# Cross-covariance attention and maxout FFN: k loaded ahead of q, norms taken during the gram, weights in halves, first v transposed on TensorE, split tail

## The chip, the cores and the metric

One core of one Trainium2 chip. The metric is the device time of one execution in microseconds (us). Each kernel ran several times on the same chip as the kernel before. The experiments were run in three calls on three chips, each beside the kernel before, which took 614.36 us beside the first four experiments, 614.28 beside the next four and 615.03 beside the last version and its base. A run's time is about 1.7 to 2.2 us longer than the span in its trace (614.43 against 612.3 us for the profiled run of the kernel before). Inside the traces I therefore compare spans and moments, and between kernels medians of the times.

The engines are PE (TensorE; PEld is its weight load), DVE (VectorE), ACT (ScalarE), POOL (GpSimd, which issues the loads here) and SP (which issues the stores and the DMA transposes). SPq is SP's queue.

## The reference, cut to what matters

```
# q, k, v: (4, 6144, 256) f32
qn = q / norm(q, axis=1);  kn = k / norm(k, axis=1)
s  = kn^T @ qn / tau                    # (4, 256, 256)
a  = softmax(s, axis=-1)
x  = v @ a                              # (4*6144, 256)
h  = max(x @ w1, x @ w2, x @ w3)        # d_ff = 768
out = h @ w_out
```

The kernel never forms x. Per batch it computes `aw_m = a @ w_m` once and then `h = max(v @ aw_m)`. So a batch needs all of q and k (the "gram") and a short chain of small operations (the softmax) before its first useful matmul on v.

## The kernel before

The parts that matter, with cuts marked (...):

```python
    make_identity(nc, ident)
    for w in [2, 2] + [4] * 10 + [2, 2]:   # q and k pieces in turn
        load_qk(0, g0, w); g0 += w
    # whole w1, w2, w3, then v0, v1, wo, v2: all on POOL's queue
    ...
def gram(b):                               # per pair of groups tp, per half j:
    # q_j x k (256 columns), q_j x q_j (128), k_j x k_j (128), all into one PSUM bank
def softmax_t(ps):
    # DVE dkm = diag(k x k) -> PE kb = ones x dkm -> ACT Ln, Exp -> rkb (1/norm of k)
    # DVE n2q = diag(q x q) -> ACT Ln, Exp -> rq
    # DVE e_in = gram * rkb -> ACT et = Exp(e_in * rq)
    ...
def v_transpose(gi):
    SP.dma_start_transpose(out=vt, in_=v_sb)

for ch in range(NCH):                      # NCH = 12 chunks of 512 tokens per batch
    load_v(gi + 3)                         # POOL; 4 v buffers
    v_transpose(gi + 2)                    # SP
    if more and 1 <= ch < 9:
        load_qk(b + 1, (ch - 1) * 6, 6)    # POOL, next batch
    for fc in range(FC):                   # 6 blocks of 128 columns of d_ff
        h_block(gi, aw, fc)                # 6 matmuls, ACT copy, two DVE max
        if ch == NCH - 1 and more and fc == 0:
            et = softmax_t(ps)
        # output matmuls of the chunk before, between the blocks
    # gram(b + 1) after chunk 10; aw of b + 1 after chunk 11
```

A block's six matmuls fill three of six PSUM banks. ACT copies the first bank to SBUF, DVE takes the maximum with the second and then with the third.

## Time and profile before

| | before |
|---|---|
| time, median of 3 | 614.6 us (614.44 to 615.2) |
| span of the trace | 612.3 us |
| PE busy | 580.5 us (95%) |
| end of the first gram (its last matmul starts at 37.12) | 37.4 us |
| first matmul on v (h_ps) | 50.13 us |
| PE idle at each of three batch boundaries | 2.1 us |

PE is busy 95% of the span. As long as its own work stays the same, time can come only from where it is idle or slow: the head, the boundaries and the tail. The first view is PE's own list of waits over the whole run: who was waited for, us in total, times, longest.

```profile
PE gram L148 <- DMA k_sb<-in_k_dram: 14.3, 12, 5.2
PE kb_ps L163 <- DVE dkm L160: 5.9, 4, 1.8
PE h_ps L237 <- DMA vt_sb<-v_sb: 3.6, 1, 3.6
PE rs_ps L193 <- ACT et L181: 2.2, 2, 2.0
PE o_ps L256 <- DVE ht_sb L242: 0.9, 1, 0.9
PE h_ps L237 <- ACT s_mx L240: 0.8, 3, 0.3
```

The first gram waits for k. The norm chain (dkm, kb) is waited for four times, once in each batch. The first transposed v costs one wait of 3.6 us, and the tail 0.9. The last line is a wait of 0.3 us at each boundary for the ACT copy (s_mx); with the 1.8 for dkm it makes up the 2.1 us of the table.

The timeline of the head shows the order (start, duration, engine, line, operation, count; in brackets the idle time before and what ended it):

```profile
37.79 0.70 PE L163 MATMUL kb_ps<-dkm,ones_f 128*128 128x256 f32 x2 [0.38 <-DVE dkm L160]
...
40.98 5.57 PE L205 MATMUL ew_ps<-w_sb,et 128*128 128x384 bf16 x24
...
43.20 8.52 SPq L225 DMA_TRANSPOSE vt_sb<-v_sb  x4
...
50.13 12.22 PE L237 MATMUL h_ps<-vt_sb,aw_sb 128*128 128x512 bf16 x48 [3.58 <-DMA vt_sb<-v_sb]
...
50.65 0.53 POOL L108 DMA_DIRECT2D v_sb<-in_v_dram  x1 [13.49 <-DMA vt_sb<-v_sb]
```

POOL stood still for 13.5 us, because the load of the fifth v tile (v4) needs the buffer of v0, which is free only when the DMA transpose of v0 has read it. The next batch's q and k loads stand behind v4 in POOL's order.

The view by stretches at the second boundary (stretch, its length, then busy us and instructions of PE, PEld, DVE, ACT and POOL, granted clock, DMA share, GB/s):

```profile
320.00:330.00 10.00, 7.90 (x45) 4.30 (x44) 7.15 (x17) 4.42 (x11) 0.00 (x0) 1.00 0.01 2
```

PE is idle for 2.1 of these 10 us. The timeline of the tail:

```profile
605.11 0.69 DVE L242 TENSOR_TENSOR ht_sb<-h_ps,s_mx 128x512 bf16<-128x512 f32 x1
...
605.86 2.25 PE L256 MATMUL o_ps<-wo_sb,ht_sb 128*128 128x256 bf16 x19 [0.86 <-DVE ht_sb L242]
...
608.14 0.60 ACT L259 ACTIVATE o_sb<-o_ps 128x512 f32<-128x512 f32 x1 [0.66 <-PE o_ps L256]
```

19 of the last 24 output matmuls run after the last ht, because the first output tile needs it and PE works in order.

### The profile page before, as it was taken

The numbers are of one execution on the slowest core, as the hardware profiler recorded it, in microseconds if no ns is written. First come the engines' busy times: TensorE is split into PE (matmuls) and PEld (weight loads), VectorE is DVE, ScalarE is ACT, GpSimd is POOL, SyncE is SP. The second block draws the span as 40 slices with busy tenths as digits, with TensorE's granted clock in tenths as the row PEclk, the third lists the DMA queues.
The fourth block names the chain that finished last, engine by engine and source line by source line (L and its number), as shares of the span: only waits on it lengthen the run. The fifth ranks groups of instructions, "written<-read, shape, count | busy, mean of one in ns | idle before, by whom it ended". The sixth has DMA issues, their size and how long they took to land. (4 is left out here: it accounts for less than half of the span.)

```text
span 612.3 us, 9533 instructions
## 1 busy us (share of the span) xinstructions
PE 580.5 (95%) x3576; PEld 351.5 (57%) x3576; DVE 409.8 (67%) x638; ACT 241.4 (39%) x433; POOL 69.6 (11%) x134
## 2 busy tenths in 40 slices
PE   3777999999989999999999999999998999999996
PEld 3753555555766555555585555555585555555554
DVE  0025778787627887877716878777735787777774
ACT  0033444444225444444405444444423544444442
POOL 6433012100100211100110211110000000000000
PEclk9988999999999999999999999999999999999999
DMA  8999999944732978854570787895440434433111
GB/s 71 105 176 147 153 96 168 155 117 87 147 43 78 127 133 127 130 114 121 101 107 35 118 127 102 146 148 102 121 87 1 109 81 87 121 69 104 53 69 70
DMA packets 77102, 65.11 MB, mean 106 GB/s; under 512 B 53504, under 2 KB 64768, under 8 KB 77056
## 3 DMA queue, kind: packets, MB, share of 16 engines
q0 software_dynamic: 19456, 26.75, 38.4%
q1 hardware_dynamic: 57600, 37.76, 24.6%
q8 instruction: 28, 0.46, 0.3%
q14 instruction: 18, 0.15, 0.1%
HBM read 78.64 MB, written 25.17 MB: 170 GB/s over the span
## 5 line engine op out<-in xcount | busy, mean ns | idle before, releaser
L237 PE MATMUL h_ps<-vt_sb,aw_sb 128*128 128x512 bf16 x1728 | 404.7, 380 | 4.4 <-DMA vt_sb<-v_sb 3.6
L241 DVE TENSOR_TENSOR s_mx<-h_ps,s_mx 128x512 bf16<-128x512 f32 x288 | 198.0, 687 | 116.3 <-ACT s_mx L240 115.2
L237 PEld LDWEIGHTS <-aw_sb 128*128 128x128 bf16 x1728 | 169.1, 98 | 172.5 <-issue 4.5
L240 ACT ACTIVATE s_mx<-h_ps 128x512 bf16<-128x512 f32 x288 | 171.1, 595 | 225.0 <-PE h_ps L237 222.9
L242 DVE TENSOR_TENSOR ht_sb<-h_ps,s_mx 128x512 bf16<-128x512 f32 x288 | 199.2, 692 | 30.0
L256 PE MATMUL o_ps<-wo_sb,ht_sb 128*128 128x256 bf16 x1152 | 155.4, 273 | 0.9 <-DVE ht_sb L242 0.9
L256 PEld LDWEIGHTS <-ht_sb 128*128 128x128 bf16 x1152 | 112.6, 98 | 51.9 <-DVE ht_sb L242 1.1
L259 ACT ACTIVATE o_sb<-o_ps 128x512 f32<-128x512 f32 x96 | 57.3, 597 | 92.1 <-PE o_ps L256 89.5
L108 POOL DMA_DIRECT2D v_sb<-in_v_dram x48 | 25.7, 536 | 443.5 <-DMA vt_sb<-v_sb 441.3
L148 PE MATMUL gram<-k_sb,q_sb 128*128 128x512 fp8e4 x192 | 56.4, 330 | 14.3 <-DMA k_sb<-in_k_dram 14.3
L152 PE MATMUL gram<-k_sb 128*128 128x256 fp8e4 x192 | 47.0, 245 | 0.0
L150 PE MATMUL gram<-q_sb 128*128 128x256 fp8e4 x192 | 46.6, 243 | 0.0
L150 PEld LDWEIGHTS <-q_sb 128*128 128x256 fp8e4 x192 | 28.0, 146 | 8.1 <-issue 7.9
L148 PEld LDWEIGHTS <-q_sb 128*128 128x256 fp8e4 x192 | 27.9, 145 | 7.2 <-DMA q_sb<-in_q_dram 6.9
L152 PEld LDWEIGHTS <-k_sb 128*128 128x256 fp8e4 x192 | 30.6, 159 | 0.0
L160 DVE TENSOR_TENSOR dkm<-gram,ident 128x128 f32<-128x128 f32 x8 | 2.0, 283 | 36.1 <-PE gram L152 36.1
L100 POOL DMA_DIRECT2D k_sb<-in_k_dram x38 | 20.9, 551 | 12.3 <-DMA k_sb<-in_k_dram 6.1
L99 POOL DMA_DIRECT2D q_sb<-in_q_dram x38 | 20.9, 551 | 8.5 <-DMA q_sb<-in_q_dram 7.1
L211 DVE TENSOR_SCALAR aw_sb<-ew_ps,rinv 128x384 bf16<-128x384 f32 x24 | 14.6, 617 | 7.0 <-PE ew_ps L205 6.4
L171 ACT ACTIVATE lnk<-kb_ps 128x256 f32<-128x256 f32 x4 | 1.5, 384 | 44.8 <-PE kb_ps L163 44.8
L205 PE MATMUL ew_ps<-w_sb,et 128*128 128x384 bf16 x96 | 18.2, 346 | 0.0
L208 ACT ACTIVATE aw_sb<-ew_ps,rinv 128x384 bf16<-128x384 f32 x24 | 13.0, 580 | 3.5 <-PE ew_ps L205 3.1
(24 smaller groups left out, 34.4 us busy)
## 6 DMA issues: line engine op xcount, KB each, us to landing
out_dram<-o_sb SPq DMA_DIRECT2D x48, 512.0 KB, 2.9
v_sb<-in_v_dram POOLq DMA_DIRECT2D x48, 256.0 KB, 3.9
q_sb<-in_q_dram POOLq DMA_DIRECT2D x24, 192.0 KB, 5.9
k_sb<-in_k_dram POOLq DMA_DIRECT2D x24, 192.0 KB, 7.6
q_sb<-in_q_dram POOLq DMA_DIRECT2D x10, 128.0 KB, 9.7
k_sb<-in_k_dram POOLq DMA_DIRECT2D x10, 128.0 KB, 9.7
w_sb<-in_moe_w_dram POOLq DMA_DIRECT2D x3, 384.0 KB, 8.6
vt_sb<-v_sb SPq DMA_TRANSPOSE x48, 3.9
```

The lines of the kernel that those rows point to most:

```text
L99: POOL.dma_start(out=qt[:, g0:g0 + w, :], in_=q_r[b][:, g0:g0 + w, :])
L100: POOL.dma_start(out=kt[:, g0:g0 + w, :], in_=k_r[b][:, g0:g0 + w, :])
L108: POOL.dma_start(out=t, in_=v_r[gi // NCH, gi % NCH])
L148: PE.matmul(ps[j][:, 0:C], lhsT=qt[:, tsl, jsl], rhs=kt[:, tsl, :], start=(tp == 0), stop=last, perf_mode=DR, skip_group_check=True)
L150: PE.matmul(ps[j][:, C:C + P], lhsT=qt[:, tsl, jsl], rhs=qt[:, tsl, jsl], start=False, stop=last, perf_mode=DR, skip_group_check=True)
L152: PE.matmul(ps[j][:, C + P:C + 2 * P], lhsT=kt[:, tsl, jsl], rhs=kt[:, tsl, jsl], start=False, stop=last, perf_mode=DR, skip_group_check=True)
L237: PE.matmul(t.rearrange("p (t n) -> p t n", t=TPC), lhsT=aw[m][:, ic, fsl], rhs=vt[:, :, ic, :], start=(ic == 0), stop=(ic == CC - 1))
L240: ACT.activation(out=s_mx, in_=hp[0], func=AF.Copy)
L241: DVE.tensor_tensor(out=s_mx, in0=hp[1], in1=s_mx, op=ALU.max)
L242: DVE.tensor_tensor(out=ht[:, fc, :], in0=hp[2], in1=s_mx, op=ALU.max)
L256: PE.matmul(st["ps"][:, half], lhsT=ht[:, fc, t * P:(t + 1) * P], rhs=wo_sb[:, fc, :], start=(fc == 0), stop=(fc == FC - 1))
L259: ACT.activation(out=st["o"][:, t - 1:t + 1, :].rearrange("p t d -> p (t d)"), in_=st["ps"], func=AF.Copy)
```

## The change

Its intent: shorten the head (k first, its norms taken while q arrives; half of the weights and the first v ahead of the rest; the first v transposed on PE; PE kept busy with matmuls on zeros during the first softmax), take the norm chain off the path at the boundaries, and shorten the tail. The diff, cut to its core:

```diff
-    for w in [2, 2] + [4] * 10 + [2, 2]:
-        load_qk(0, g0, w)
+    for load, widths in ((load_k, [4, 4] + [8] * 5), (load_q, [8] * 5 + [4, 2, 2])):
+        ... # identity made after the first two k loads
+    load_w(0)          # left halves of w1, w2, w3
     load_v(0)
+    load_w(1)          # right halves
     load_v(1)
@@ gram
+        kk = htile("kk")
+        for tp in range(NG // 2):      # all k x k first
+            ...
+        # DVE: dkm = diag(kk)
         ps = [xtile(f"gram{j}") for j in range(CC)]
         for tp in range(NG // 2):      # q x k and q x q only
+            if tp == 11:
+                # PE kb = ones x dkm; ACT Ln, Exp -> rkb
+        return ps, rkb
@@ softmax_t: n2q, rq, e_in, et only
+    def v_transpose_pe(gi):
+        vt_ps = xtile("vt_ps", cols=TPC * C, dtype=BF16)
+        for i in range(TPC * CC):
+            PE.matmul(vt_ps[...], lhsT=v_sb[...], rhs=ident, is_transpose=True, ...)
+        ACT.activation(...)            # copy the first half to vt
+        DVE.tensor_copy(...)           # and the second
@@ head
-    v_transpose(0)
-    v_transpose(1)
     ps = gram(0)
-    et = softmax_t(ps)
+    for i in range(8):
+        PE.matmul(warm_ps, lhsT=ident, rhs=warm, ...)      # zeros
+    et = softmax_t(*ps)
     rinv = rowsums(et)
-    aw_half(et, rinv, aw, 0)
-    aw_half(et, rinv, aw, 1)
+    aw_half(et, rinv, aw, 0, [2], lambda: v_transpose_pe(0))
+    v_transpose(1)
@@ chunk 0
+    gaps[0].insert(0, lambda: aw_half(et, rinv, aw, 1))    # after block 0
@@ tail
-    for f in pending:
-        f()
+    o_last(B * NCH - 1)   # 20 matmuls on blocks 0..4 first, then 4 on block 5;
+                          # ACT and DVE copy, stores from ACT and SP
```

More of the change, by code (lines that the diff above doesn't have):

```diff
@@ L95, in alloc_qk, with load_k, load_q @@
                  qk_pool.tile([P, NG, C], FP8, name="k_sb", tag="k"))
-    def load_qk(b, g0, w):
-        qt, kt = qk[b]
-        POOL.dma_start(out=qt[:, g0:g0 + w, :], in_=q_r[b][:, g0:g0 + w, :])
-        POOL.dma_start(out=kt[:, g0:g0 + w, :], in_=k_r[b][:, g0:g0 + w, :])
+    def load_k(b, g0, w):
+        POOL.dma_start(out=qk[b][1][:, g0:g0 + w, :], in_=k_r[b][:, g0:g0 + w, :])
+    def load_q(b, g0, w):
+        POOL.dma_start(out=qk[b][0][:, g0:g0 + w, :], in_=q_r[b][:, g0:g0 + w, :])
     v_tiles = {}
@@ L109, in load_v, with load_w @@
         v_tiles[gi] = t
-    ident = consts.tile([P, P], BF16, name="ident")
-    make_identity(nc, ident)
     alloc_qk(0)
-    g0 = 0
-    for w in [2, 2] + [4] * 10 + [2, 2]:
-        load_qk(0, g0, w)
-        g0 += w
-    w_sb = []
-    for i, w in enumerate(w_list):
-        wt = consts.tile([P, CC, d_ff], BF16, name=f"w{i}_sb")
-        POOL.dma_start(out=wt, in_=w.rearrange("(cc p) f -> p cc f", p=P))
-        w_sb.append(wt)
+    for load, widths in ((load_k, [4, 4] + [8] * 5), (load_q, [8] * 5 + [4, 2, 2])):
+        g0 = 0
+        for w in widths:
+            load(0, g0, w)
+            g0 += w
+            if load is load_k and g0 == 8:
+                ident = consts.tile([P, P], BF16, name="ident")
+                make_identity(nc, ident)
+    w_sb = [consts.tile([P, CC, d_ff], BF16, name=f"w{i}_sb") for i in range(3)]
+    def load_w(fh):
+        fsl = slice(fh * FH, (fh + 1) * FH)
+        for wt, w in zip(w_sb, w_list):
+            POOL.dma_start(out=wt[:, :, fsl], in_=w.rearrange("(cc p) f -> p cc f", p=P)[:, :, fsl])
+    load_w(0)
     load_v(0)
+    load_w(1)
     load_v(1)
@@ L134 @@
     DVE.memset(ones_c, 1.0)
+    warm = consts.tile([P, CHUNK], BF16, name="warm")
+    DVE.memset(warm, 0.0)
     neg_ln_tau = -math.log(float(tau)) if float(tau) != 1.0 else 0.0
@@ L141, in gram @@
         qt, kt = qk[b]
+        kk = htile("kk")
+        for tp in range(NG // 2):
+            tsl = slice(2 * tp, 2 * tp + 2)
+            for j in range(CC):
+                jsl = slice(j * P, (j + 1) * P)
+                PE.matmul(kk[:, jsl], lhsT=kt[:, tsl, jsl], rhs=kt[:, tsl, jsl], start=(tp == 0 and j == 0),
+                          stop=(tp == NG // 2 - 1), perf_mode=DR, skip_group_check=True)
+        dkm = sm.tile([P, C], FP32, name="dkm")
+        for j in range(CC):
+            jsl = slice(j * P, (j + 1) * P)
+            DVE.tensor_tensor(out=dkm[:, jsl], in0=kk[:, jsl], in1=ident, op=ALU.mult)
         ps = [xtile(f"gram{j}") for j in range(CC)]
@@ L151, in gram, with softmax_t @@
                           start=False, stop=last, perf_mode=DR, skip_group_check=True)
-                PE.matmul(ps[j][:, C + P:C + 2 * P], lhsT=kt[:, tsl, jsl], rhs=kt[:, tsl, jsl],
-                          start=False, stop=last, perf_mode=DR, skip_group_check=True)
-        return ps
-    def softmax_t(ps):
-        dkm = sm.tile([P, C], FP32, name="dkm")
-        for j in range(CC):
-            DVE.tensor_tensor(out=dkm[:, j * P:(j + 1) * P], in0=ps[j][:, C + P:C + 2 * P],
-                              in1=ident, op=ALU.mult)
-        kb_ps = htile("kb_ps")
-        PE.matmul(kb_ps[:, :C], lhsT=ones_f, rhs=dkm, start=True, stop=True)
+            if tp == 11:
+                kb_ps = htile("kb_ps")
+                PE.matmul(kb_ps[:, :C], lhsT=ones_f, rhs=dkm, start=True, stop=True)
+                lnk = sm.tile([P, C], FP32, name="lnk")
+                rkb = sm.tile([P, C], FP32, name="rkb")
+                ACT.activation(out=lnk, in_=kb_ps[:, :C], func=AF.Ln)
+                ACT.activation(out=rkb, in_=lnk, func=AF.Exp, scale=-0.5)
+        return ps, rkb
+    def softmax_t(ps, rkb):
         n2q = sm.tile([P, CC], FP32, name="n2q")
@@ L168, in softmax_t @@
                                      op0=ALU.mult, op1=ALU.add, accum_out=n2q[:, j:j + 1])
-        lnk = sm.tile([P, C], FP32, name="lnk")
-        rkb = sm.tile([P, C], FP32, name="rkb")
-        ACT.activation(out=lnk, in_=kb_ps[:, :C], func=AF.Ln)
-        ACT.activation(out=rkb, in_=lnk, func=AF.Exp, scale=-0.5)
         lnq = sm.tile([P, CC], FP32, name="lnq")
@@ L196, in rowsums, with aw_half @@
         return rinv
-    def aw_half(et, rinv, aw, fh):
+    def aw_half(et, rinv, aw, fh, at=(), between=None):
         fsl = slice(fh * FH, (fh + 1) * FH)
@@ L213, in aw_half, with vt_tile @@
                 n += 1
+                if n in at:
+                    between()
     vts = {}
     hts = {}
+    def vt_tile(gi):
+        vts[gi] = vt_pool.tile([P, TPC, CC, P], BF16, name="vt_sb")
+        return vts[gi].rearrange("p t cc n -> p (t cc) n")
     def v_transpose(gi):
@@ L223, in v_transpose @@
         v_sb = v_tiles.pop(gi)
-        vt = vt_pool.tile([P, TPC, CC, P], BF16, name="vt_sb")
-        SP.dma_start_transpose(out=vt.rearrange("p t cc n -> p (t cc) n"),
-                               in_=v_sb.rearrange("p t c -> p (t c)"))
-        vts[gi] = vt
+        SP.dma_start_transpose(out=vt_tile(gi), in_=v_sb.rearrange("p t c -> p (t c)"))
+    def v_transpose_pe(gi):
+        v_sb = v_tiles.pop(gi).rearrange("p t c -> p (t c)")
+        vt = vt_tile(gi)
+        vt_ps = xtile("vt_ps", cols=TPC * C, dtype=BF16)
+        for i in range(TPC * CC):
+            PE.matmul(vt_ps[:, i * P:(i + 1) * P], lhsT=v_sb[:, i * P:(i + 1) * P], rhs=ident,
+                      is_transpose=True, start=(i == 0), stop=(i == CC * TPC - 1))
+        half = TPC * CC // 2
+        ps = vt_ps.rearrange("p (i n) -> p i n", n=P)
+        ACT.activation(out=vt[:, :half, :], in_=ps[:, :half, :], func=AF.Copy)
+        DVE.tensor_copy(out=vt[:, half:, :], in_=ps[:, half:, :])
     def h_block(gi, aw, fc):
@@ L265, in o_steps, with o_last @@
         return [lambda t=t: step(t) for t in range(TPC)]
-    v_transpose(0)
-    v_transpose(1)
+    def o_last(gi):
+        ht = hts[gi]
+        o_sb = o_pool.tile([P, TPC, d_model], FP32, name="o_sb")
+        pss = [xtile("o_ps") for _ in range(TPC // 2)]
+        for fcs in (range(FC - 1), (FC - 1,)):
+            for t in range(TPC):
+                half = slice((t % 2) * d_model, (t % 2 + 1) * d_model)
+                for fc in fcs:
+                    PE.matmul(pss[t // 2][:, half], lhsT=ht[:, fc, t * P:(t + 1) * P], rhs=wo_sb[:, fc, :],
+                              start=(fc == 0 and t % 2 == 0), stop=(fc == FC - 1), skip_group_check=True)
+        dst = out_r[gi // NCH, gi % NCH]
+        o0 = o_sb[:, 0:2, :].rearrange("p t d -> p (t d)")
+        o1 = o_sb[:, 2:4, :].rearrange("p t d -> p (t d)")
+        ACT.activation(out=o0, in_=pss[0], func=AF.Copy)
+        DVE.tensor_copy(out=o1, in_=pss[1])
+        ACT.dma_start(out=dst[:, 0:2, :], in_=o_sb[:, 0:2, :])
+        SP.dma_start(out=dst[:, 2:4, :], in_=o_sb[:, 2:4, :])
     ps = gram(0)
-    et = softmax_t(ps)
+    warm_ps = htile("warm_ps")
+    for i in range(8):
+        PE.matmul(warm_ps, lhsT=ident, rhs=warm, start=(i == 0), stop=(i == 7))
+    et = softmax_t(*ps)
     aw = alloc_aw()
     rinv = rowsums(et)
-    aw_half(et, rinv, aw, 0)
-    aw_half(et, rinv, aw, 1)
+    aw_half(et, rinv, aw, 0, [2], lambda: v_transpose_pe(0))
+    v_transpose(1)
     pending = []
@@ L287 @@
             if more and 1 <= ch < 9:
-                load_qk(b + 1, (ch - 1) * 6, 6)
+                load_k(b + 1, (ch - 1) * 6, 6)
+                load_q(b + 1, (ch - 1) * 6, 6)
             gaps = [[] for _ in range(FC)]
@@ L293 @@
                 place = [1, 2, 3, 4]
+            if gi == 0:
+                gaps[0].insert(0, lambda: aw_half(et, rinv, aw, 1))
             for s, f in enumerate(pending):
@@ L298 @@
                 if ch == NCH - 1 and more and fc == 0:
-                    et = softmax_t(ps)
+                    et = softmax_t(*ps)
                 for f in gaps[fc]:
```

## The prediction

> **What bounds the kernel now.** The part table of the profile gives PE 580.5 of 612.3 us (95%), so only head, batch boundaries and tail can give. The stretches view: from 56 us on PE is full except for 2.1 us in each of three boundary stretches (7.90 of 10 us busy).
>
> *Head, DMA-bound.* From 10 us the 16 DMA engines are full at about 104 GB/s written as fp8, which is 416 GB/s read as f32; the Trainium skill, "DMA: Bandwidth & Descriptors" (Specifications), gives 435 GB/s as fabric ceiling, so bytes cannot land faster. Last k lands at 36.3 us (issue list, issue plus time to landing), gram ends 37.1. Timeline: dkm, kb, rkb, e_in, et take until 40.98; 24 weight matmuls to 46.6; PE waits 3.6 us for the first transposed v (v lands 43.2, transpose lands 50.1); h starts 50.13. Clock: matmuls of 512 columns are 0.43 us apart until 54.4, then 0.216; weight matmuls 0.32 until 43.8, then 0.16. This agrees with the Trainium skill, "TensorE: Matmul & The Clock Gate" (Part 1): half rate until some 3.4 us of activity, again after an idle window.
>
> **What the change does.**
> 1. First load issued about 0.6 us earlier (identity no longer ahead). q and k land about 35.4.
> 2. Head gram: after k only q work remains per q piece, 2.7 us cold (0.335 per pair of matmuls), 1.3 us warm, against 2.5 us of transfer. PE keeps up, probably turns warm; gram ends about 36.
> 3. The norm chain (dkm, kb, Ln, Exp) leaves the path: gram end to first weight matmul falls from 3.9 to about 2.2 us. The eight zero matmuls fit in if warm (1.7 us), not if cold (3.4).
> 4. Half the weights plus first v land about 39.7 instead of 43.2; the PE transposes wait there about 0.7 us, cost about 0.8, and replace 6.9 us of DMA transpose. First h about 42; the second weight half (1.95 us) moves behind its first block.
> 5. Estimate for the start of chunk 1: 60.9 before, 52 to 52.8 after (DVE, 1.39 us per block plus three 0.62 us evictions, and the still DMA-transposed v1 both limit there). Head gain about 8 us.
> 6. Boundaries: kb (0.5 us) moves into the gram, the wait for it (1.8) goes, but the second block's ACT copy still stands behind n2q, rq, et: a PE wait of about 1.5 us stays. Net about 0.95 us each, 2.9 in three.
> 7. Tail: 20 of 24 output matmuls run before the last ht; ACT and DVE copy in parallel. About 1.1 us.
>
> Sum 12 us; I take off half a microsecond for the chance that PE stays cold in the q phase. Predicted **603.0 us**, range 599.8 to 606.5. Faster by over 2% (below 602.3): 0.42; within 2%: 0.57; slower: 0.01.
>
> **What would show it.** Step 2: gram end at 35.5 to 36.5, q-phase spacing falling to 0.16 per pair. Step 3: 2.0 to 2.4 us to the first row-sum or weight matmul, weight matmuls 0.16 apart from the start. Step 4: first h at 41 to 43 us, at 0.216. Step 5: chunk 1 at 51.5 to 53. Step 6: the wait of PE for dkm gone from the waits view; a wait for the ACT copy of 1.2 to 1.7 us in its place, three times. Step 7: last output copy ends near 607.7 less the gain above. PE busy time of the main loop unchanged.
>
> **What would make it wrong.** The clock falls back between q pieces (half-busy PE), making zero matmuls and weights cold: 2 to 3 us lost. Half-row weight loads (1.5 KB reads) running slower than 0.42 MB/us. The v1 transpose, beside full queues, landing after 53. A boundary with no remaining wait: 4 us more gained.

## The result, and the profile after

The median is 606.43 us (606.05 to 607.15, 4 runs) against 614.67 us before (4 runs). The ratio is 0.9866, 95% interval 0.9849 to 0.9883. Ratios here are the mean time of one kernel's fast runs over that of the other's in the same rounds, so they are not quite the ratio of the medians. The change is faster by 1.3%, within 2%, and 606.43 lies just inside the predicted range (599.8 to 606.5). The gain is 8.2 us where 11.7 was predicted.

PE's waits of the changed kernel:

```profile
PE kk L156 <- DMA k_sb<-in_k_dram: 13.6, 7, 5.2
PE h_ps L267 <- DMA vt_sb<-v_sb: 3.8, 1, 3.8
PE gram L168 <- DMA q_sb<-in_q_dram: 3.7, 4, 1.6
PE h_ps L267 <- ACT s_mx L270: 3.5, 3, 1.2
PE vt_ps L252 <- DVE aw_sb L226: 0.7, 1, 0.7
PE rs_ps L208 <- ACT et L196: 0.2, 1, 0.2
```

The waits for kb and et are gone, and three waits for the ACT copy took kb's place. But a wait of 3.8 us for a transposed v is still there. It has moved to v1, as the timeline shows:

```profile
36.14 1.90 PE L320 MATMUL warm_ps<-warm,ident 128*128 128x512 bf16 x8
...
38.47 0.81 PE L220 MATMUL ew_ps<-w_sb,et 128*128 128x384 bf16 x4
...
39.95 0.62 PE L252 MATMUL vt_ps<-ident,v_sb 128*128 128x128 bf16 x8 [0.67 <-DVE aw_sb L226]
...
40.86 0.53 POOL L109 DMA_DIRECT2D v_sb<-in_v_dram  x1 [1.40 <-PE vt_ps L252]
...
41.71 1.45 PE L267 MATMUL h_ps<-vt_sb,aw_sb 128*128 128x512 bf16 x6
...
44.11 10.93 SPq L245 DMA_TRANSPOSE vt_sb<-v_sb  x3
...
44.95 6.64 PE L267 MATMUL h_ps<-vt_sb,aw_sb 128*128 128x512 bf16 x30
...
55.34 4.07 PE L267 MATMUL h_ps<-vt_sb,aw_sb 128*128 128x512 bf16 x12 [3.76 <-DMA vt_sb<-v_sb]
```

Up to 41.71 us the head went as intended: the first matmul on v starts 8.4 us earlier than before. The 30 matmuls that finish chunk 0 end at 51.59, and then PE stands still until 55.34. The transpose of v1, started at 44.11, took 11.2 us to land by the issue list. In the kernel before, the transpose of v0 took 6.9. POOL's line at 40.86 is the counterpart of the one at 50.65 before: v4, and behind it k and q of the next batch, now go out 9.8 us earlier, because v0's buffer was freed by PE.

The stretches after that wait:

```profile
52.00:54.00 2.00, 0.00 (x0) 0.00 (x0) 1.16 (x2) 0.00 (x0) 0.00 (x0) 1.00 1.33 97
54.00:56.00 2.00, 0.66 (x3) 0.31 (x4) 0.00 (x0) 0.01 (x1) 0.15 (x1) 1.00 1.18 208
56.00:58.00 2.00, 2.00 (x8) 0.82 (x7) 1.28 (x2) 0.84 (x2) 2.00 (x5) 0.66 0.62 104
58.00:60.00 2.00, 2.00 (x8) 0.99 (x7) 1.34 (x3) 0.34 (x1) 2.00 (x4) 0.50 1.09 148
```

The granted clock (the third number from the right) is 0.66 and then 0.50: the idle time also cost PE its clock, some 1.3 us after PE had started again (an estimate from the 0.66). In the traces of the first three experiments below, where PE has no such wait, the clock reads 1.00 in the same stretches. Twelve matmuls from 55.34 to the next group at 59.20 took 3.86 us, where at 0.216 us apart they take 2.59. This agrees with the Trainium skill, "TensorE: Matmul & The Clock Gate" (Part 1), which says that an idle window of about 3.4 us brings the clock back to half. In two traces further down (the versions without matmuls on zeros) the clock fell after waits of no more than 1.7 us, so 3.4 us is not to be taken as a wait that is always safe.

The second boundary now lies in two stretches. Together PE is idle for 1.2 us in them, against 2.1 before (10.00 and 7.90 busy). After it, the tail:

```profile
310.00:320.00 10.00, 9.62 (x83) 7.22 (x82) 2.55 (x8) 2.45 (x7) 1.06 (x2) 1.00 0.60 67
320.00:330.00 10.00, 9.21 (x64) 5.91 (x64) 8.34 (x14) 5.75 (x11) 0.00 (x0) 1.00 0.10 42
```

```profile
598.39 2.78 PE L306 MATMUL o_ps<-wo_sb,ht_sb 128*128 128x256 bf16 x24
...
599.21 0.69 DVE L272 TENSOR_TENSOR ht_sb<-h_ps,s_mx 128x512 bf16<-128x512 f32 x1
601.04 0.60 ACT L311 ACTIVATE o_sb<-o_ps 128x512 f32<-128x512 f32 x1 [2.66 <-issue]
601.21 0.69 DVE L312 COPY o_sb<-o_ps 128x512 f32<-128x512 f32 x1 [1.31 <-PE o_ps L306]
```

The 24 output matmuls run as one stretch, without waiting for the last ht (599.90). With three moments that both traces have, the gain in span, 6.9 us, divides as follows:

| moment | before | after | gain so far | gain of the part |
|---|---|---|---|---|
| second group of output matmuls in chunk 1 (head) | 64.14 | 61.58 | 2.56 | 2.56 |
| end of the last ht (boundaries) | 605.80 | 599.90 | 5.90 | 3.34 |
| end of span (tail) | 612.3 | 605.4 | 6.9 | 1.0 |

The head gave 2.6 us, although the first matmul on v came 8.4 us earlier. That is the question for the experiments.

### The profile page after: what moved, and what is told of

Its sections match the earlier page's. It is cut to its first block, busy times and chain, and to the rows that moved or that the text cites. A ratio compares the mean times of both kernels' runs of the same rounds, so it can differ in the third digit from the quotient of the medians.

```text
span 605.4 us, 9558 instructions
## 1 busy us (share of the span) xinstructions
PE 575.6 (95%) x3592; PEld 346.2 (57%) x3592; DVE 410.0 (68%) x641; ACT 241.6 (40%) x433; POOL 64.9 (11%) x124
## 3 DMA queue, kind: packets, MB, share of 16 engines
q1 hardware_dynamic: 56544, 37.23, 25.9%
## 4 chain that ended last, share of the span: by engine, by line
PE 89%; DMA 8%; ACT 1%; POOL 1%; issue 0%; DVE 0%; POOLq 0%
PE h_ps L267 60%; PE o_ps L286 20%; DMA q_sb<-in_q_dram 3%; PE gram L168 3%; PE ew_ps L220 2%; DMA vt_sb<-v_sb 2%; DMA k_sb<-in_k_dram 2%; PE kk L156 2%; DMA v_sb<-in_v_dram 1%; PE gram L170 1%; ACT et L196 0%; PE o_ps L306 0%; POOL k_sb L98 0%; ACT s_mx L270 0%; PE kb_ps L174 0%
## 5 line engine op out<-in xcount | busy, mean ns | idle before, releaser
L286 PE MATMUL o_ps<-wo_sb,ht_sb 128*128 128x256 bf16 x1128 | 152.8, 273 | 0.0
L286 PEld LDWEIGHTS <-ht_sb 128*128 128x128 bf16 x1128 | 110.7, 98 | 50.8 <-issue 0.6
L168 PE MATMUL gram<-k_sb,q_sb 128*128 128x512 fp8e4 x192 | 35.8, 287 | 3.7 <-DMA q_sb<-in_q_dram 3.7
L170 PE MATMUL gram<-q_sb 128*128 128x256 fp8e4 x192 | 34.1, 224 | 0.0
L156 PE MATMUL kk<-k_sb 128*128 128x256 fp8e4 x192 | 20.0, 269 | 13.6 <-DMA k_sb<-in_k_dram 13.6
L168 PEld LDWEIGHTS <-q_sb 128*128 128x256 fp8e4 x192 | 27.1, 141 | 4.9 <-DMA q_sb<-in_q_dram 4.8
L156 PEld LDWEIGHTS <-k_sb 128*128 128x256 fp8e4 x192 | 18.1, 145 | 15.3 <-DMA k_sb<-in_k_dram 14.8
L170 PEld LDWEIGHTS <-q_sb 128*128 128x256 fp8e4 x192 | 26.1, 136 | 0.2
L161 DVE TENSOR_TENSOR dkm<-kk,ident 128x128 f32<-128x128 f32 x8 | 2.0, 285 | 27.5 <-PE kk L156 27.5
L101 POOL DMA_DIRECT2D q_sb<-in_q_dram x32 | 17.6, 553 | 11.3 <-DMA k_sb<-in_k_dram 11.0
L98 POOL DMA_DIRECT2D k_sb<-in_k_dram x31 | 17.1, 554 | 0.8 <-POOLq L386 0.8
## 6 DMA issues: line engine op xcount, KB each, us to landing
k_sb<-in_k_dram POOLq DMA_DIRECT2D x5, 256.0 KB, 11.2
```

Source lines behind the costliest of these rows:

```text
L101: POOL.dma_start(out=qk[b][0][:, g0:g0 + w, :], in_=q_r[b][:, g0:g0 + w, :])
L156: PE.matmul(kk[:, jsl], lhsT=kt[:, tsl, jsl], rhs=kt[:, tsl, jsl], start=(tp == 0 and j == 0), stop=(tp == NG // 2 - 1), perf_mode=DR, ski ...
L168: PE.matmul(ps[j][:, 0:C], lhsT=qt[:, tsl, jsl], rhs=kt[:, tsl, :], start=(tp == 0), stop=last, perf_mode=DR, skip_group_check=True)
L170: PE.matmul(ps[j][:, C:C + P], lhsT=qt[:, tsl, jsl], rhs=qt[:, tsl, jsl], start=False, stop=last, perf_mode=DR, skip_group_check=True)
L286: PE.matmul(st["ps"][:, half], lhsT=ht[:, fc, t * P:(t + 1) * P], rhs=wo_sb[:, fc, :], start=(fc == 0), stop=(fc == FC - 1))
```

## The experiments

Theory A: the head's gain was lost to the transpose of v1, by an idle wait and by the clock that fell with it. Its cause (A1) is contention: the early loads of v4, k and q share the DMA engines with the transpose. Rivals: (A2) the transpose is slow by itself or in its issue; (B) DVE or the DMA queues limit chunk 1 in any case.

### Transposing v1 on TensorE too

```diff
-    v_transpose(1)
+                gaps[1].insert(0, lambda: v_transpose_pe(1))   # chunk 0, after block 1
```

> Changed kernel with the second v tile (v1) also transposed on TensorE, after block 1 of chunk 0. Theory A (the head's gain was eaten by the DMA transpose of v1, which landed at 55.3 us and left PE idle 3.8 us and then at half clock): chunk 1 starts at 52.0 to 52.6 us, matmuls of 512 columns stay 0.216 us apart, the time falls from 606.4 to 601.0 to 602.5 us. Rival B (DVE or the full DMA queues limit chunk 1 anyway): chunk 1 starts after 54 us and the time stays above 604.5 us.

Measured: 601.55 us (601.24 to 601.82), ratio to before 0.9787, interval 0.9771 to 0.9803. PE's wait for vt is gone. The second output group of chunk 1 starts at 55.86 us instead of 61.58. Chunk 1 starts near 51.3 (24 matmuls of chunk 0 at 0.216 us after 46.14), somewhat earlier than I wrote. Rival B falls: with v1 there, neither DVE nor the queues hold chunk 1 back.

### Holding the early loads back

With three v buffers, v3 takes v0's buffer and v4 has to wait for v1's, so that k and q behind v4 wait as well:

```diff
-    v_pool = ctx.enter_context(tc.tile_pool(name="v", bufs=4))
+    v_pool = ctx.enter_context(tc.tile_pool(name="v", bufs=3))
```

> Changed kernel with three v buffers instead of four, so that the load of the fifth v and the first k and q pieces of the next batch are issued only after the DMA transpose of v1. Theory A1 (the transpose is slow, 11.2 us, because those loads, which the change issues at 40.9 to 42.6 us, share the DMA engines with it): transpose of v1 lands within 6 to 8 us of its start at 44.1, PE waits under 0.7 us for it, time 601 to 603 us. Rival A2 (the transpose is slow by itself or in its issue): it still takes over 10 us, time 606 us or above.

The second, weaker dose leaves v4 early and starts only k and q one chunk later:

```diff
-            if more and 1 <= ch < 9:
-                load_k(b + 1, (ch - 1) * 6, 6)
-                load_q(b + 1, (ch - 1) * 6, 6)
+            if more and 2 <= ch < 10:
+                load_k(b + 1, (ch - 2) * 6, 6)
+                load_q(b + 1, (ch - 2) * 6, 6)
```

> Changed kernel with the k and q pieces of the next batch starting in chunk 2 instead of 1; the fifth v is still loaded early. Theory A1: 1.57 MB less of reading stands beside the transpose of v1, so it lands 1.5 to 4 us earlier than 55.2 us, PE's wait falls from 3.8 us to between 0 and 2.3 us, time 601.5 to 605 us. Rival A2: no difference in the landing, time 606 us.

| version | early loads beside v1's transpose | v1's transpose, us to land | PE's wait for it | time, us |
|---|---|---|---|---|
| changed kernel | v4, k, q | 11.2 | 3.8 | 606.43 |
| k, q one chunk later | v4 | 6.9 | none | 601.06 |
| three v buffers | none | 5.6 | none | 601.39 |

The times of the last two are medians of 4 runs (600.89 to 602.47 and 600.85 to 602.43). The loads sent before v4 (w_out, v2 and v3) are still under way beside the transpose in all three; with three buffers v3 goes out 1.3 us later (40.18 instead of 38.92). The transpose gets shorter as loads are taken away, and nothing about the transpose itself was changed. That is A1, and A2 falls. The shares of DMA time by queue from 44 to 55 us show the same. Here q0 is the queue of POOL's loads and q1 that of the transposes (packets, MB, share of the 16 engines' time). First the changed kernel, then the version with three buffers:

```profile
q0 software_dynamic: 916, 1.27, 81.1%
q1 hardware_dynamic: 1544, 0.39, 36.2%
```

```profile
q0 software_dynamic: 692, 1.04, 62.0%
q1 hardware_dynamic: 3168, 0.79, 61.5%
```

In the same 11 us the transposes moved 0.39 MB beside the early loads and 0.79 MB where these were held back to 49.55 us. The Trainium skill, "DMA: Bandwidth & Descriptors" (Queues, rings and completion order), says that each DMA engine goes round between the queues that have work, packet by packet. From 48 to 52 us the trace of the changed kernel agrees:

```profile
q0 software_dynamic: 282, 0.40, 95.6%
q1 hardware_dynamic: 282, 0.07, 13.0%
```

Each queue moved 282 packets, but those of the transposes are much smaller, so they got 0.07 of 0.47 MB. One transpose has 1056 packets (a third of the 3168 above), so in these 4 us it got through a quarter. When the loads were done it went faster: 534 packets from 54.5 to 55 us. The turns are not the whole difference: the transposes' first packets come 3.9 us after the issue in the changed kernel (48.0) and 2.9 us after it with three buffers (46.3), and why they start late is not shown. The sum, 11.2 against 5.6 us, only these runs tell.

And the head with three buffers (start, duration and count, as before; POOL's line is its first load after v3):

```profile
43.43 5.89 SPq L245 DMA_TRANSPOSE vt_sb<-v_sb  x3
...
44.27 9.23 PE L267 MATMUL h_ps<-vt_sb,aw_sb 128*128 128x512 bf16 x42
...
49.55 0.53 POOL L109 DMA_DIRECT2D v_sb<-in_v_dram  x1 [8.82 <-DMA vt_sb<-v_sb]
```

42 matmuls run without a gap from chunk 0 into chunk 1. The second output group of chunk 1 starts at 55.28 instead of 61.58, 6.3 us earlier. Its parts: 0.7 because the first matmul on v comes at 41.02 instead of 41.71 in this trace, 3.9 for the wait (51.43 to 55.34, the first being 30 matmuls of 0.216 us after 44.95), and 1.7 for the clock (from the start of chunk 1 to that group 6.24 us instead of 4.53). The medians of the times differ by 5.0 us; the profiled run of the changed kernel was the slowest of its four, and that of the three-buffer version the fastest of its four. The 0.7 is no effect of the buffers that could be shown: in the eleven traces with the new head the last matmul of the first gram starts anywhere between 35.27 and 36.34 us.

### The matmuls on zeros

```diff
-    for i in range(8):
-        PE.matmul(warm_ps, lhsT=ident, rhs=warm, start=(i == 0), stop=(i == 7))
```

> Changed kernel without the eight matmuls on zeros. Theory C (they keep the clock up through the first softmax): PE is idle some 1.9 us after the gram and the weight matmuls may fall to 0.32 us apart, so that first h comes up to 2 us later; but chunk 1 waits for the transposed v1 until 55.3 us in any case, so the time moves by under 0.5 us, at most 1.0. Rival D (they are needed for the measured gain): the time rises by over 1.5 us.

Measured: 608.49, 609.29, 604.55 and 604.19 us (clock 0.992, 0.994, 0.997, 0.997), against 606.05 to 607.15 with zeros. The median, 606.52, did not move, but the runs fell into two groups, some 2 us on either side of it. So this run decides nothing about their worth, and why two runs without zeros beat all four with them stays open. The trace is of a run in the slow group. Compared with the trace with zeros, it did not lose in the head. Its clock did fall during the softmax (to 0.50 from about 37.4 us, after a wait of 1.68), but its gram had ended 0.8 us earlier, and the first matmul on v came at 41.69, as with zeros (41.71). Its loss came after the wait for v1 (4.0 us here): all twelve matmuls ran at half the clock, 5.09 us from 55.60 to the next group instead of 3.86, and the second output group of chunk 1 came at 62.94 instead of 61.58. The price of the clock after that wait was 2.8 us in this trace and 1.7 in that of the changed kernel, so part of the spread of these runs need not come from the zeros at all. I repeated it where no wait for v1 hides the result, on the version with three buffers:

> The three-buffer version (601.4 us, no wait for v1) without the eight matmuls on zeros. Theory C (zeros keep the clock up; with the v1 wait gone nothing hides a slow start): some executions have the weight matmuls at 0.32 us, first h comes 0.5 to 1.5 us later, median 601.5 to 603 us, with a wider spread than with zeros. Rival D2 (they are worth nothing): median and spread unchanged within 0.5 us.

Measured: 602.99, 600.83, 603.27 and 600.84 us (clock 0.996, 0.998, 0.996, 1.0), median 601.91, against 600.85 to 602.43 with zeros. Again there are two groups, at 600.8 and 603.1. The trace, of a slow run, shows where most of its 2 us went. First PE in it, then the same matmuls in the version with zeros:

```profile
39.81 1.04 PE L252 MATMUL vt_ps<-ident,v_sb 128*128 128x128 bf16 x8 [0.67 <-DMA v_sb<-in_v_dram]
40.64 2.68 PE L220 MATMUL ew_ps<-w_sb,et 128*128 128x384 bf16 x8
```

```profile
39.26 0.62 PE L252 MATMUL vt_ps<-ident,v_sb 128*128 128x128 bf16 x8 [0.67 <-DVE aw_sb L226]
39.72 1.46 PE L220 MATMUL ew_ps<-w_sb,et 128*128 128x384 bf16 x8
```

Eight weight matmuls took 2.68 us instead of 1.46, and the eight transposes 1.04 instead of 0.62. That is 1.6 of the 2.1 us by which the first matmul on v came later (43.15 instead of 41.02); the other 0.5 is a gram that ended later. The clock fell between 39.5 and 40 us (0.68 there, 0.50 after), when PE had waited 1.68 us for et and then 0.67 for v0; the first four weight matmuls, between these waits, still ran at full speed. Without zeros this may be a matter of chance from run to run (two of four); none of the nine traces with zeros shows it. The trace fits theory C, but the times do not establish it: the difference of the medians, 0.5 us, is within the spread, and the version with zeros spreads by 1.6 us itself. If the slow group is the clock, the zeros are worth about 2 us in half of the runs, so about 1 on the mean at most.

### The parts that worked, each undone

Both are on the version with three buffers (601.39 us). It was run on another chip. For the later batches, the gram and the norm chain in the old order:

```diff
-                ps = gram(b + 1)
+                ps = gram_old(b + 1)     # q x k, q x q, k x k together; dkm, kb, Ln, Exp in softmax_t
```

> The three-buffer version, but in the three later batches the gram and the norm chain in the order of the kernel before. Theory E (early k norms are worth about 1.1 us at each boundary, because a wait of PE for the ACT copy of 1.2 us replaces that for dkm and kb of 2.1 us in all): PE idle 2.1 us per boundary again, time 3.0 to 3.6 us longer, 604.4 to 605.0. Rival F (worth the whole wait, 2 us each): 6 us longer, 607.5.

Measured: 604.97 us (604.37 to 605.34), 3.6 us longer. PE's three waits for dkm are back (5.5 us in total), and those for the ACT copy fall from 3.5 to 0.8. Theory E holds: 1.2 us for each boundary, not the whole wait.

The old tail:

```diff
-    o_last(B * NCH - 1)
+    for f in pending:
+        f()
```

> The three-buffer version with the tail of the kernel before. Theory G: the split tail is worth 1.0 us: last ht to end of span 6.5 us instead of 5.5, time 602.4 us. Rival: no difference, because the store's 2.9 us to landing rule the end.

Measured: 602.55 us (602.1 to 603.12), 1.2 us longer. From the end of the last ht (593.78) to the end of the span (600.3) it is 6.5 us instead of 5.5. Theory G holds.

### Going further: the wait that replaced the norm chain

PE still waits three times for ACT's copy of block 1, which stands behind et in ACT's order. The softmax at the boundaries is cut in three, so that no copy waits behind an operation that is not ready:

```diff
+    if ch == NCH - 1 and more and fc == 0:  n2q                      # DVE
+    if ch == NCH - 1 and more and fc == 1:  Ln, Exp of n2q; e_in     # ACT; DVE
+    if ch == NCH - 1 and more and fc == 2:  et                       # ACT
-    if ch == NCH - 1 and more and fc == 0:  et = softmax_t(*ps)
```

> The three-buffer version with the softmax at the boundaries cut in three: n2q after block 0, Ln, Exp of q norms and e_in after block 1, et after block 2, so that the ACT copy of block 1 no longer stands behind et. If that copy is what PE waits for (1.17 us, three times), the wait falls to under 0.4 us each and the time by 2.0 to 3.2 us, to 598.2 to 599.4. If DVE, with 1.4 us of softmax work between the blocks, is the limit, the wait only moves and the time stays within 0.8 us of 601.4.

Measured: 597.10 us (596.51 to 597.47), 4.3 us less than 601.39 (measured in another call) and more than I had expected. PE's waits are now:

```profile
PE kk L156 <- DMA k_sb<-in_k_dram: 13.6, 7, 5.5
PE gram L168 <- DMA q_sb<-in_q_dram: 3.3, 3, 1.8
PE vt_ps L270 <- DMA v_sb<-in_v_dram: 0.4, 1, 0.4
PE rs_ps L226 <- ACT et L206: 0.2, 1, 0.2
```

Nothing is left after the head. At the first boundary the first output group comes at 172.43 instead of 173.50 us, although this trace's head was 0.33 us later: 1.4 us. The idle time of 1.18 us in the waits view is short by the end of the matmul in the pipe (1.35 us from where the next matmul could have started, 170.80, to where it did, 172.15). Three times 1.4 is 4.2, which is close to the measured gain; the spans of the two traces differ by 3.9. I had counted 1.17 and expected a remainder; there was none.

The last version puts v0 ahead of the first weight half, and its transposes in the place of three of the zero matmuls:

```diff
+    load_v(0)
     load_w(0)
-    load_v(0)
     load_w(1)
...
-    for i in range(8):  # zeros
+    for i in range(5):  # zeros
     et = softmax_t(*ps)
+    # PE transposes of v0 here, their ACT and DVE copies after the row sums' reciprocal
     rinv = rowsums(et)
-    aw_half(et, rinv, aw, 0, [2], lambda: v_transpose_pe(0))
+    aw_half(et, rinv, aw, 0)
```

> The split-softmax version (597.1 us) with v0 loaded ahead of the first weight half, its PE transposes in the place of three of the eight zero matmuls, ahead of the row sums, and its copies after et. If the head is still held by the wait for v0 and by the transposes between the weight matmuls (0.4 plus 0.5 us), first h comes 0.6 to 0.9 us earlier and the time falls by as much. If the third weight half, which now lands last, holds the weight matmuls instead, the gain is under 0.4 us.

> The split-softmax version again, as the base of this call: 597.1 us within 0.7.

Measured: 595.79 us (595.6 to 596.27, 5 runs) against 597.24 (596.43 to 597.31, 4 runs) for its base. Its ratio to the kernel before is 0.9688, interval 0.9673 to 0.9704. PE runs through from the zeros to the first matmul on v:

```profile
36.96 0.61 PE L274 MATMUL vt_ps<-ident,v_sb 128*128 128x128 bf16 x8
...
38.19 2.11 PE L238 MATMUL ew_ps<-w_sb,et 128*128 128x384 bf16 x12
40.14 1.46 PE L292 MATMUL h_ps<-vt_sb,aw_sb 128*128 128x512 bf16 x6
```

The first matmul on v comes at 40.14 instead of 41.58 us in its base's trace, 1.4 us earlier and more than expected. 0.3 us of that is an earlier start of the zeros (36.09 against 36.41); the remainder is the wait and the transposes that no longer stand between the weight matmuls. This is the best version: 10.6 us faster than the changed kernel and 19 us faster than the kernel before.

## Why the prediction was right or wrong, point by point

The time was inside the range, at its edge, and the most likely outcome (within 2%) came true. That the number held was partly luck: 606.43 is 0.07 us from the edge, and one of the four runs (607.15) lies outside. In span the change gave 6.9 us instead of the 12 of the sum, and one term failed.

- **Step 1, q and k land about 35.4 us.** The last q piece's matmuls start at 35.75. Right, though not for the reason given: the first load starts at 1.23 instead of 1.42 us, 0.2 and not 0.6 earlier. The loads also ran a little faster than before (107 GB/s written on the mean from 10 to 32 us, against 105), where the prediction had taken the rate as fixed.
- **Step 2, gram ends about 36, clock full in the q phase.** It ended at 36.30, and the spacing of a pair fell from 0.32 to 0.17 us at 25.9. Right.
- **Step 3, 2.2 us from the gram to the first weight matmul.** 36.30 to 38.47, 2.2 us. Right. Measured in the same way, from the end of the last gram matmul, it was 3.6 before and not 3.9. The zeros fit in (36.14 to 38.04).
- **Step 4, wait for v0 about 0.7, transposes 0.8, first h about 42.** 0.67, 0.62 and 41.71, at full clock. Right. (The view puts the 0.67 down to a DVE copy that ended at 39.93; the weight load of the same transposes waited for v0 until 39.94, and three other traces put the wait down to v0's load, among them the one without zeros shown above.)
- **Step 5, chunk 1 at 52 to 52.8, head gain about 8.** This is the step that failed. Chunk 1 started at 55.34, and the head gain was 2.56 us. The prediction listed a late v1 among the risks but took it as held at 52 to 52.8. From the start of the transpose (44.11) that leaves it 7.9 to 8.7 us; it took 11.2. Nothing in the prediction says that freeing v0's buffer 10 us earlier lets POOL send v4, k and q at just that time. It also left out the price of the clock, 1.7 us. DVE, the other limit that it named, did not hold: with v1 transposed on PE, chunk 1 started at 51.3. With the loads held back, the head is worth 8.9 us (64.14 to 55.28). The estimate of the moment before was off as well: chunk 1 had started near 59.6 (12 matmuls of 0.216 us before 62.19), not at 60.9. That would have lowered the term by 1.3.
- **Step 6, about 0.95 us at each boundary, with a wait of 1.2 to 1.7 for the ACT copy in place of the one for dkm.** The wait was 1.18 and the gain 3.34 in three, 3.6 in the run that undid it. Right in mechanism, a little low in size.
- **Step 7, tail 1.1 us.** 1.0 in the traces, 1.2 in the run that undid it. Right.

Shown by runs: the transpose's contention with the early loads (two doses), the worth of the boundaries and of the tail, and the wait behind et. Open: what the zeros are worth, the two groups of times without them, why two of those runs beat all runs with zeros in the changed kernel, and why the transposes' first packets start late.

## What to carry to other kernels

When a change frees a buffer earlier, look for the queue that was waiting for it: here an in-order load queue was let go 10 us early, and its loads doubled the time of the one transfer that the next stage needed. Moving a limit forward exposes the next transfer in line, so cost that one under the load it will meet, and add the price of the clock where PE stands still (1.7 and 2.8 us here, after waits of 3.8 and 4.0; waits of 1.7 us were followed by a fall too, in two traces without zeros). In an in-order engine, place each part of a chain where its input is ready, so that a copy that frees PSUM banks never stands behind it; that was worth more here (4.3 us) than taking the norms early (3.6).

## What the Trainium skill lacked or had wrong

- "DMA: Bandwidth & Descriptors" (Queues, rings and completion order; DMA Transpose) tells that queues take turns, but not what that does to a DMA transpose beside loads. One 128 x 1024 bf16 tile (256 KB) took 11.2 us beside three more early loads, 6.9 beside one and 5.6 beside none of the three. With equal packets (282 and 282 in 4 us) the loads moved 0.40 MB and the transposes 0.07.
- "TensorE: Matmul & The Clock Gate" (Part 4) says that the full clock does not engage for transposes, at 275 to 390 ns for a 128 x 128 one. Here eight in a row took 0.62 us in all when they followed matmuls at full clock, and 1.04 where the clock had fallen. From the first to the next instruction that is 57 ns each (39.26 to 39.72) and 104 ns each (39.81 to 40.64), so in these traces they do follow the granted clock. The page's figures are for single transposes, which these are not.
- The same page (Part 1) does not say whether matmuls on zeros keep the clock up. With them, all nine traces have the weight matmuls at full speed. Without them, two of four runs were longer than the other two in both versions (by 4.5 and 2.3 us), and both traces show the clock fallen, after waits of no more than 1.7 us.
- The same page (Part 1) says that clock records can be unreliable, but not in what way they fail here: the granted clock of the changed kernel reads 1.00 from 20 to 30 us, while the gram's pairs went from 0.32 to 0.17 us apart at 25.9. The spacing of matmuls is the safer sign.
